# Second chunk's first k and v sums ahead of the raw weight loads, first chunk's loads joined, three high halves on VectorE

## The chip, the cores and the metric

One core of a Trainium2 chip runs the program. TensorE multiplies, VectorE (DVE) and ScalarE (ACT) do elementwise work and reductions, GpSimd (POOL) does some of it and issues accumulating DMAs, SyncE (SP) issues most other DMAs. Every engine works through its own instructions in the order in which they were written out, and waits where one needs something that is not there yet. The metric is the device time of one execution in microseconds; the median of three runs is 759.44 us (757.23 to 761.62).

## The reference

Three layers on 4 sequences of 576 positions, 8 heads of 64 features (512 in all), fp32:

```python
# attention, twice, added
q_d, k_d, v_d = (t.reshape(B, H, 144, 4, D).mean(axis=3) for t in (q, k, v))
out_d = softmax(q_d @ k_d.T / 8) @ v_d                  # every 4th position
out_up = np.repeat(out_d, 4, axis=2)
mask = np.abs(pos[:, None] - pos[None, :]) < 4
out_local = softmax(np.where(mask, q @ k.T / 8, -1e9)) @ v
x = (out_up + out_local).reshape(B, S, 512)
# feed-forward with a norm
xn = (x - mean) / np.sqrt(var + 1e-6) * g_ln
x = x + np.maximum(xn @ w_ch1, 0) @ w_ch2               # 512 -> 2048 -> 512
# mixing with the previous position
k = np.maximum((mu_k * x + (1 - mu_k) * x_prev) @ w_k, 0)   # 512 -> 1024
r = sigmoid((mu_r * x + (1 - mu_r) * x_prev) @ w_r)
out = r * (k * k @ w_v)
```

The sums over four positions (k_d, v_d, q_d without the factor) are the "sums" of this document.

## The kernel before

The 2304 positions are cut into six chunks of 384. For each chunk the attention runs in four units, one for each pair of heads (`hp` 0 to 3; `units` lists them as (chunk, hp)), then the norm, then the feed-forward in 16 blocks of 128 hidden features: `emit_l1` fills a bank `h_ps`, `split_h` writes `hh` (ScalarE, L663) and `hl` (VectorE, L664), `emit_l2` adds into four banks `acc`. While chunk c is in the feed-forward, the units of chunk c+1 are woven in between (`Attn`, `slot`). After six chunks the mixing layer follows. Each fp32 product is made of three passes over high and low parts (`mm3`, L290 to L292).

Weights arrive as raw 64-bit numbers (`raw`, L122, 512 KB a DMA) and are turned into fp32 and then into a high part `w_..h` and a low part `w_..l`. `conv_gen` does this piece by piece: A (two ScalarE passes, L80 and L81), D (one VectorE pass, L83), H (the high half, L86, a copy on ScalarE unless the piece's number stands in `BY_VECTOR`), L (the low half, L89, VectorE). Pieces 0 and 1 are the first quarter of `w1`, 2 and 3 of `w2`, 4 and 5 the second quarter of `w1`, 6 and 7 of `w2`, 8 and 9 the third of `w1`, 10 and 11 of `w2`. Four fetches of two DMAs each run ahead (`AHEAD`).

The first chunk is done by hand, as two pairs of head pairs (`pair(0)`, `pair(1)`) in an order given by the string `FIRST`: a digit is a step of that pair, a dot four idle matmuls, `a` and `b` the v sums, A, D, H, L with a number weight steps, `n` a step of the norm. Its k comes whole (`kf`) and is summed on VectorE (L832), its v comes as four raw rows (`vr_01`) and is summed in L779 and L781.

The later chunks' sums are made by DMAs (`sums`): the first quarter of a k sum `kd` and of a v sum `vd` is loaded by SP, then GpSimd issues three adding DMAs on top, each after the one before has landed (L335, L336). The second chunk needs sums of sequence 1; its units 0 and 1 had theirs issued in step `q` of `FIRST`, after four fetches of raw weights, with their q, k and v loads. A `scd` matmul (L393) multiplies `kd` by the summed q, `sc` (L397) is the windowed score.

Completion of DMAs from SP and ScalarE is told over eight lanes taken in turn (`DMAHW0` to `DMAHW7` in the orders below), and an issue waits for the DMA that had its lane before.

## Time and profile before

| | us |
|---|---|
| median of three runs | 759.44 |
| the profiled execution | 759.42 |
| its span, first to last instruction | 757.6 |
| TensorE busy | 731.2 |
| VectorE busy | 438.8 |
| ScalarE busy | 375.7 |
| GpSimd busy | 106.3 |

The profile is one execution. Its page gives busy times and shares, 40 slices of the span, queues, the chain that ended last and the costliest groups; the trace behind it answers for any stretch with a timeline, lists of waits, windows and DMA queues. A row of a timeline ends with the idle time ahead of it and what ended that, in brackets. Matmuls overlap, so their durations add up to more than the distance of their starts.

### The profile page before, as it was taken

The numbers are of one execution on the slowest core, as the hardware profiler recorded it, in microseconds if no ns is written. First come the engines' busy times: TensorE is split into PE (matmuls) and PEld (weight loads), VectorE is DVE, ScalarE is ACT, GpSimd is POOL, SyncE is SP. The second block draws the span as 40 slices with busy tenths as digits, with TensorE's granted clock in tenths as the row PEclk, the third lists the DMA queues.
The fourth block names the chain that finished last, engine by engine and source line by source line (L and its number), as shares of the span: only waits on it lengthen the run. The fifth ranks groups of instructions, "written<-read, shape, count | busy, mean of one in ns | idle before, by whom it ended". The sixth has DMA issues, their size and how long they took to land.

```text
span 757.6 us, 13995 instructions
## 1 busy us (share of the span) xinstructions
PE 731.2 (97%) x5472; PEld 708.7 (94%) x5472; DVE 438.8 (58%) x820; ACT 375.7 (50%) x782; POOL 106.3 (14%) x141
## 2 busy tenths in 40 slices
PE   4869999999999999999999999999999999999998
PEld 3658899999999999999999999999999999999998
DVE  4986987755475556645675554547797355143211
ACT  1887975535254343544355344236888576411100
POOL 3044200500063404510300020002000000000000
PEclk8798999999999999999999999999999999999999
DMA  9899653464538754755332346906725628695311
GB/s 272 284 305 270 163 152 102 106 205 138 171 98 197 185 165 119 162 136 182 126 111 102 99 131 220 353 33 208 259 105 187 205 94 310 230 295 183 106 63 53
DMA packets 76306, 130.43 MB, mean 172 GB/s; under 512 B 8464, under 2 KB 53136, under 8 KB 74576
## 3 DMA queue, kind: packets, MB, share of 16 engines
q1 hardware_dynamic: 65456, 118.97, 47.7%
q0 software_dynamic: 9920, 9.25, 6.9%
q10 hardware_dynamic: 864, 1.32, 0.6%
q8 instruction: 43, 0.70, 0.4%
q14 instruction: 23, 0.19, 0.1%
HBM read 89.13 MB, written 40.37 MB: 171 GB/s over the span
## 4 chain that ended last, share of the span: by engine, by line
PE 86%; DMA 8%; ACT 4%; issue 0%; SPq 0%; DVE 0%; POOL 0%; DVEq 0%; ACTq 0%
PE b_ps L1166 10%; PE acc L290 9%; PE h_ps L290 8%; PE acc L292 8%; PE acc L291 8%; PE h_ps L291 8%; PE h_ps L292 8%; PE b_ps L291 7%; PE b_ps L290 7%; PE b_ps L292 7%; DMA kd<-in_kr 3%; PE av L469 2%; DMA q<-in_qw 2%; PE sc L397 1%; PE scd L393 1%; DMA vd<-in_vr 1%
## 5 line engine op out<-in xcount | busy, mean ns | idle before, releaser
L663 ACT ACTIVATE hh<-h_ps 128x384 fp32r<-128x384 f32 x96 | 47.0, 490 | 111.9 <-PE h_ps L292 107.4
L664 DVE SCALAR_TENSOR_TENSOR hl<-h_ps,hh 128x384 fp32r<-128x384 f32 x96 | 53.0, 553 | 81.0 <-ACT hh L663 80.4
L1166 PE MATMUL b_ps<-xk,wk 128*128 128x384 f32 x504 | 88.3, 335 | 0.2 <-DVE u L1138 0.2
L1166 PEld LDWEIGHTS b_ps<-xk,wk 128*128 128x128 f32 x504 | 87.3, 188 | 0.8 <-DVE u L1138 0.5
L698 POOL TENSOR_TENSOR x<-x2t,x 128x384 f32<-128x384 f32 x24 | 24.1, 1022 | 296.7 <-DVE x2t L697 296.5
L290 PE MATMUL b_ps<-ko,wv 128*128 128x384 f32 x192 | 64.1, 334 | 0.0
L291 PE MATMUL b_ps<-ko,wv 128*128 128x384 f32 x192 | 64.1, 334 | 0.0
L292 PE MATMUL b_ps<-ko,wv 128*128 128x384 f32 x192 | 64.1, 334 | 0.0
L1292 DVE TENSOR_TENSOR rin<-b_ps,rin 128x384 f32<-128x384 f32 x24 | 13.3, 557 | 61.4 <-PE b_ps L292 60.2
L335 POOL DMA_DIRECT2D kd<-in_kr x36 | 36.4, 1015 | 70.5 <-DMA kd<-in_kr 70.0
L336 POOL DMA_DIRECT2D vd<-in_vr x36 | 37.1, 1032 | 36.3 <-DMA vd<-in_vr 28.2
L83 DVE SCALAR_TENSOR_TENSOR rm<-rm,raw 128x512 uint32<-128x512 uint32 (+1 forms) x40 | 33.7, 844 | 9.3 <-ACT raw L81 9.0
L1218 ACT CAST ko<-kin 128x1536 fp32r<-128x1536 f32 x12 | 17.6, 1478 | 38.9 <-PE b_ps L291 22.9
L291 PEld LDWEIGHTS b_ps<-ko,wv 128*128 128x128 f32 x192 | 36.0, 188 | 0.0
L290 PEld LDWEIGHTS b_ps<-ko,wv 128*128 128x128 f32 x192 | 36.0, 188 | 0.0
L292 PEld LDWEIGHTS b_ps<-ko,wv 128*128 128x128 f32 x192 | 36.0, 188 | 0.0
L80 ACT ACTIVATE rm<-raw 128x512 f32<-128x512 f32 (+1 forms) x40 | 32.6, 815 | 4.1 <-DMA raw<-in_w 1.8
L1220 DVE TENSOR_TENSOR ko<-kin,ko 128x1536 fp32r<-128x1536 f32 x12 | 20.9, 1754 | 23.0 <-ACT ko L1218 22.9
L290 PE MATMUL acc<-hh,w_0h 128*128 128x384 f32 x96 | 33.3, 347 | 0.2 <-ACT w_0h L86 0.2
L290 PE MATMUL acc<-hh,w_1h 128*128 128x384 f32 x96 | 33.4, 348 | 0.0
L290 PE MATMUL h_ps<-ah,w_2h 128*128 128x384 f32 x96 | 33.3, 347 | 0.0
L291 PE MATMUL acc<-hl,w_0h 128*128 128x384 f32 x96 | 32.7, 340 | 0.0
(221 smaller groups left out, 2087.0 us busy)
## 6 DMA issues: line engine op xcount, KB each, us to landing
raw<-in_w SPq DMA_DIRECT2D x32, 512.0 KB, 7.1
kd<-k SPq DMA_DIRECT2D x48, 192.0 KB, 2.1
kin<-kd SPq DMA_DIRECT2D x12, 768.0 KB
wk<-wkd SPq DMA_DIRECT2D x7, 1024.0 KB, 9.4
v<-in_vw SPq DMA_DIRECT2D x20, 256.0 KB, 3.3
rd<-r SPq DMA_DIRECT2D x24, 192.0 KB, 1.9
rin<-rd SPq DMA_DIRECT2D x24, 192.0 KB, 2.6
out<-rin SPq DMA_DIRECT2D x24, 192.0 KB, 3.2
```

Of the source, the lines that this page charges most:

```text
L80: in_order(pinned, nc.scalar.activation(ru.bitcast(F32), high.bitcast(F32), AF.Prelu, scale=-2.0 ** -80, alpha=-2.0 ** -32))
L83: in_order(pinned, nc.vector.scalar_tensor_tensor(ru, ru, 3, low.bitcast(U32), op0=ALU.logical_shift_left, op1=ALU.bitwise_or))
L290: nc.tensor.matmul(ps, wh, ah, start=first, stop=False)
L291: nc.tensor.matmul(ps, wh, al, start=False, stop=False)
L292: nc.tensor.matmul(ps, wl, ah, start=False, stop=last)
L335: in_order(r > 0, eng.dma_start(kd, kr[b, hp, r], **op))
L336: in_order(r > 0, eng.dma_start(vd, vr[b, hp, r], **op))
L663: nc.scalar.activation(hh, ps[:, 0:N], AF.Relu)
L664: last_hl[0] = nc.vector.scalar_tensor_tensor(hl, ps[:, 0:N], 0.0, hh.bitcast(F32), op0=ALU.max, op1=ALU.subtract)
L698: nc.gpsimd.tensor_tensor(x[:, o, :], t, x[:, o, :], op=ALU.add)
L1166: nc.tensor.matmul(ps, a, m[:, k, :], start=start and k + i == 0, stop=k == nk - 1 and i == 2, skip_group_check=True)
L1220: nc.vector.tensor_tensor(l, t[g], h.bitcast(F32), op=ALU.subtract)
```

## The change

The first chunk's q, v and raw v come with one DMA for two head pairs in place of two; `vr` lies in memory with the four raw rows of a position side by side, so that a partition's load is one run of 4 KB. Both pairs' q and k are issued before the mask and the small vectors. The first sums of the second chunk's units 0 and 1 (SP's first quarters and GpSimd's adds) are issued behind the first pair's v and raw v and in front of the raw weights; their q and k loads stand between the second and third fetch of raw weights, and v behind the fourth. Step `q` is gone from `FIRST`. GpSimd's memsets are reordered. The high halves of pieces 5, 8 and 10 are copied by VectorE.

```diff
--- before.py
+++ after.py
@@ -164,6 +164,7 @@
 
         for _ in range(AHEAD):
             fetch()
+            yield
         yield step
         for n in range(len(keys) + 1):
             for ops in ((("H", n - 1), ("A", n)), (("L", n - 1), ("D", n))):
@@ -333,7 +334,7 @@
             for b, kd, vd in new:
                 eng, op = (nc.gpsimd, {"accum_op": ALU.add}) if r else (nc.sync, {})
                 in_order(r > 0, eng.dma_start(kd, kr[b, hp, r], **op))
-                in_order(r > 0, eng.dma_start(vd, vr[b, hp, r], **op))
+                in_order(r > 0, eng.dma_start(vd, vr[b, hp, :, r], **op))
             if new:
                 yield True
 
@@ -760,19 +761,17 @@
 
     def load_pair(pr):
         b = sets[pr]
+        in_order(True, nc.sync.dma_start(b["q"], qw[2 * pr:2 * pr + 2, :, 0:NG].rearrange("i p n w -> p i n w")))
         for i in range(2):
-            in_order(True, nc.sync.dma_start(b["q"][:, i], qw[2 * pr + i, :, 0:NG]))
             in_order(True, nc.scalar.dma_start(b["kf"][:, i], kf[0, 2 * pr + i]))
 
     def load_pair_v(pr):
-        for i in range(2):
-            in_order(True, nc.sync.dma_start(sets[pr]["v"][:, i], vw[2 * pr + i, :, 0:NG]))
+        in_order(True, nc.sync.dma_start(sets[pr]["v"], vw[2 * pr:2 * pr + 2, :, 0:NG].rearrange("i p n h d -> p i n h d")))
 
     vr_01 = [block(2048)[0].rearrange("p (i r f) -> p i r f", i=2, r=4) for _ in range(2)]
 
     def load_pair_vr(pr):
-        for i in range(2):
-            in_order(True, nc.sync.dma_start(vr_01[pr][0:KD, i].rearrange("p r (t d) -> p r t d", t=2), vr[0, 2 * pr + i].rearrange("r p t d -> p r t d")))
+        in_order(True, nc.sync.dma_start(vr_01[pr][0:KD].rearrange("p i r f -> p i (r f)"), vr[0, 2 * pr:2 * pr + 2].rearrange("i p r t d -> p i (r t d)")))
 
     def value_sums(pr):
         t = vr_01[pr][0:KD]
@@ -781,13 +780,10 @@
             in_order(True, nc.vector.tensor_tensor(vdt[0, 2 * pr + i].rearrange("p t d -> p (t d)"), t[:, i, 0], t[:, i, 1], op=ALU.add))
 
     load_pair(0)
+    load_pair(1)
     nc.scalar.dma_start(mask_t, mask)
     for hp in range(NHP):
         sum_tiles(0, hp)
-    for h in range(2):
-        p = slice(64 * h, 64 * h + 64)
-        for i in range(2):
-            nc.gpsimd.memset(kz[i][p, 1 - h], 0.0)
     for b in sets:
         nc.vector.memset(b["qd"][:, :, :, QB:64], 0.0)
         nc.gpsimd.memset(b["P"], 0.0)
@@ -796,19 +792,28 @@
     nc.vector.memset(one, 1.0 / DM)
     nc.scalar.copy(ones_r, one)
     make_identity(nc, ident)
-    load_pair(1)
-    nc.scalar.dma_start(vec_t, vec)
-    for pr in range(2):
-        load_pair_v(pr)
-        load_pair_vr(pr)
-    by_hand = next(conv)
+    load_pair_v(0)
+    load_pair_vr(0)
+    for h in range(2):
+        p = slice(64 * h, 64 * h + 64)
+        for i in range(2):
+            nc.gpsimd.memset(kz[i][p, 1 - h], 0.0)
+            nc.gpsimd.memset(qdz[i][p, :, 1 - h], 0.0)
     for b in sets:
         nc.gpsimd.memset(b["PT"], 0.0)
-    for i in range(2):
-        for h in range(2):
-            p = slice(64 * h, 64 * h + 64)
-            nc.gpsimd.memset(qdz[i][p, :, 1 - h], 0.0)
     nc.gpsimd.memset(PT, 0.0)
+    nc.scalar.dma_start(vec_t, vec)
+    for _ in zip(*[sums(*units[NHP + i]) for i in range(2)]):
+        pass
+    load_pair_v(1)
+    load_pair_vr(1)
+    for n in range(AHEAD):
+        next(conv)
+        if n == 1:
+            for i in range(2):
+                load_qk(*units[NHP + i])
+    load_v(*units[NHP])
+    by_hand = next(conv)
     xt[0] = xp.tile([128, NHP, N], F32, tag="x", name="x")
 
 
@@ -950,12 +955,6 @@
             warm(4)
         elif o == "W":
             warm(WARM, W1[0][0][:, 0, :], 512)
-        elif o == "q":
-            for i in range(2):
-                load_qk(*units[NHP + i])
-            for _ in zip(*[sums(*units[NHP + i]) for i in range(2)]):
-                pass
-            load_v(*units[NHP])
         else:
             next(steps[o], None)
 
@@ -1299,7 +1298,7 @@
 AHEAD = 4
 PINNED = 4
 UB = 2
-BY_VECTOR = ()
+BY_VECTOR = (5, 8, 10)
 PRE = 3
 SB = 8
 KB = 5
@@ -1313,7 +1312,7 @@
 PROB = 800
 PRO0 = 10
 GAP = -1
-FIRST = "0 0 1 1 . . . . 0 0 a 1 0 0 0 1 b A0 0 1 1 D0 1 0 0 H0 1 0 1 A1 A2 1 L0 1 D1 q n W H1 n L1 n D2"
+FIRST = "0 0 1 1 . . . . 0 0 a 1 0 0 0 1 b A0 0 1 1 D0 1 0 0 H0 1 0 1 A1 A2 1 L0 1 D1 n W H1 n L1 n D2"
 EARLY = 0
 IDLE = 2
 WARM = 8
@@ -1338,7 +1337,7 @@
     vwin = vp[:, :, idx, :].reshape(B, NHP, 2, 6, 4, 32, D)
     vwin[..., WIN:, :] = 0
     vwin = vwin.transpose(1, 4, 5, 0, 3, 2, 6).reshape(NHP, 128, 6 * B, 2, D)
-    vr = v.reshape(B, NHP, 2, 2, KD, 4, D).transpose(0, 1, 5, 4, 3, 2, 6).reshape(B, NHP, 4, KD, 2, 128)
+    vr = v.reshape(B, NHP, 2, 2, KD, 4, D).transpose(0, 1, 4, 5, 3, 2, 6).reshape(B, NHP, KD, 4, 2, 128)
     kr = k.transpose(0, 1, 3, 2).reshape(B, NHP, 128, SD, 4).transpose(0, 1, 4, 2, 3)
     vec = np.stack([np.asarray(inputs[n]).reshape(KT, 128).T for n in ("moe_g_ln", "moe2_mu_k", "moe2_mu_r")], axis=1)
```

SP's queue at the start of the program, before. `first_114` and `first_115` are the blocks of the first and second pair (q and k), `first_116` holds v of both, `first_121` and `first_122` raw v. Behind the last row stand six more raw loads, then six loads of q and k, and then the first two `kd`.

```order
L764 DMA first_114<-in_qw 128x416 x2
L764 DMA first_115<-in_qw 128x416 x2
L769 DMA first_116<-in_vw 128x512
L769 DMA first_116<-in_vw 128x512 [waits DMAHW0_49]
L775 DMA first_121<-in_vr 72x4x256 [waits DMAHW2_49]
L775 DMA first_121<-in_vr 72x4x256 [waits DMAHW5_49]
L769 DMA first_116<-in_vw 128x512 [waits DMAHW6_49]
L769 DMA first_116<-in_vw 128x512 [waits DMAHW7_49]
L775 DMA first_122<-in_vr 72x4x256 [waits DMAHW0_49]
L775 DMA first_122<-in_vr 72x4x256 [waits DMAHW1_49]
L122 DMA raw_166<-in_w1 128x1024 [waits DMAHW2_49]
L122 DMA raw_166<-in_w1 128x1024 [waits DMAHW3_49]
```

SP's queue at the same place, now, up to the first load of raw weights:

```order
L764 DMA first_114<-in_qw 128x2x416
L764 DMA first_115<-in_qw 128x2x416
L769 DMA first_116<-in_vw 128x2x512
L774 DMA first_121<-in_vr 72x2x1024
L336 DMA kd_165<-in_kr 128x144 [waits DMAHW2_49]
L337 DMA vd_166<-in_vr 72x256 [waits DMAHW3_49]
L336 DMA kd_169<-in_kr 128x144 [waits DMAHW4_49]
L337 DMA vd_170<-in_vr 72x256 [waits DMAHW5_49]
L769 DMA first_116<-in_vw 128x2x512 [waits DMAHW6_49]
L313 DMA q_193<-in_qw 128x416 [waits DMAHW7_49]
L774 DMA first_122<-in_vr 72x2x1024 [waits DMAHW0_49]
L122 DMA raw_187<-in_w1 128x1024 [waits DMAHW1_49]
```

The four first quarters `kd_165`, `vd_166`, `kd_169` and `vd_170` have moved from behind the eight raw loads to the fifth to eighth place; the second pair's v and raw v moved behind them.

ScalarE's queue of loads at the start, before: `first_114` and `first_115` take the k of the two pairs.

```order
L765 DMA first_114<-in_kf 128x579 x2
L784 DMA mask_t_101<-in_mask 128x240
L797 CAST ones_r_83<-one_146 128x128 [waits DVE_49]
L765 DMA first_115<-in_kf 128x579 [waits DMAHW1_49]
L765 DMA first_115<-in_kf 128x579 [waits DMAHW3_49]
```

And now:

```order
L766 DMA first_114<-in_kf 128x579 x2
L766 DMA first_115<-in_kf 128x579 x2
L784 DMA mask_t_101<-in_mask 128x240 [waits DMAHW0_49]
L793 CAST ones_r_83<-one_144 128x128 [waits DVE_49]
L805 DMA vec_t_81<-in_vec 128x12 [waits DMAHW1_49]
```

The second pair's k stands in front of the mask and waits for no earlier DMA; the mask waits for the first q.

VectorE around the second chunk's first unit, before (`w1_1h` and `w1_1l` are the second quarter of `w1`, `sm`, `mx`, `P`, `T` belong to the unit's softmax):

```order
L423 TENSOR_SCALAR sm_708<-sm_708 96x2
L516 TENSOR_TENSOR sum_l_1494<-xc_580,sum_h_1493 128x384
L424 RECIPROCAL mx_707<-sm_708 96x2 [waits DVE_49]
L429 TENSOR_REDUCE sm_708<-P_112 128x8 [waits Activation_49]
L83 SCALAR_TENSOR_TENSOR rm_799<-rm_799,raw_607 128x1024 [waits DMAHW5_49,DMAHW4_49]
L430 RECIPROCAL mx_707<-sm_708 128x8 [waits DVE_49]
L89 TENSOR_TENSOR w1_1l_665<-rm_666,w1_1h_664 128x1024 [waits Activation_49]
L432 TENSOR_TENSOR P_112<-P_112,mx_707 128x8x30 [waits DVE_49]
L444 STREAM_TRANSPOSE T_790<-P_112 128x256 [waits DVE_49]
```

And now:

```order
L424 TENSOR_SCALAR sm_702<-sm_702 96x2
L86 CAST w1_1h_658<-rm_660 128x1024 [waits DVE_49]
L425 RECIPROCAL mx_701<-sm_702 96x2 [waits DVE_49]
L430 TENSOR_REDUCE sm_702<-P_112 128x8 [waits Activation_49]
L351 TENSOR_REDUCE qdz1_111<-q_197 64x2x48 [waits DMAHW7_49]
L431 RECIPROCAL mx_701<-sm_702 128x8 [waits DVE_49]
L351 TENSOR_REDUCE qdz1_111<-q_197 64x2x48
L433 TENSOR_TENSOR P_112<-P_112,mx_701 128x8x30 [waits DVE_49]
L89 TENSOR_TENSOR w1_1l_659<-rm_660,w1_1h_658 128x1024
L445 STREAM_TRANSPOSE T_784<-P_112 128x256 [waits DVE_49]
```

The cast of piece 5 stands on VectorE behind the unit's sum, in front of the reciprocals, the low half and the transpose; the next unit's q sums (`qdz1_111`) moved in front of the transpose, and the pass `sum_l` behind it.

## Rows read from the trace of the kernel before

**Rows 1.** Busy table of the page, whole run: us (share) xcount per engine

```profile
PE 731.2 (97%) x5472; PEld 708.7 (94%) x5472; DVE 438.8 (58%) x820; ACT 375.7 (50%) x782; POOL 106.3 (14%) x141
```

**Rows 2.** TensorE's waits, whole run: us in total, times, longest us

```profile
PE scd L840 <- DVE kd L832: 10.4, 3, 7.3
PE scd L393 <- DMA kd<-in_kr: 5.8, 1, 5.8
```

**Rows 3.** Timeline, VectorE, 0 to 62: start us, us, operation [idle before, releaser]

```profile
7.84 0.94 DVE L828 TENSOR_REDUCE first<-first 128x192 f32<-128x768 f32 x1
...
12.02 0.76 DVE L832 TENSOR_REDUCE kd<-first 128x144 f32<-128x576 f32 x1 [3.24 <-DMA first<-in_kf]
...
13.90 0.75 DVE L832 TENSOR_REDUCE kd<-first 128x144 f32<-128x576 f32 x1 [1.12 <-DMA first<-in_kf]
...
17.54 1.21 DVE L779 TENSOR_TENSOR first<-first 72x1024 f32<-72x1024 f32 x1
...
58.93 0.45 DVE L403 TENSOR_REDUCE mx<-scd 96x2 f32<-96x288 f32 x1 [5.03 <-PE scd L393]
```

**Rows 4.** Timeline, TensorE, 51 to 81 us

```profile
51.85 0.41 PE L393 MATMUL scd<-kd,qdz 128*96 128x144 f32 x2
...
58.10 0.79 PE L393 MATMUL scd<-kd,qdz 128*96 128x144 f32 x2 [5.84 <-DMA kd<-in_kr]
...
61.87 0.41 PE L290 MATMUL h_ps<-ah,w_0h 128*128 128x384 f32 x1
...
78.46 0.69 PE L393 MATMUL scd<-kd,qdz 128*96 128x144 f32 x4
...
79.63 0.44 PE L292 MATMUL h_ps<-ah,w_1l 128*128 128x384 f32 x1
...
80.95 0.33 PE L290 MATMUL acc<-hh,w_1h 128*128 128x384 f32 x1
```

**Rows 5.** Windows: length, busy us of PE, PEld, DVE, ACT, POOL, clock, DMA, GB/s

```profile
52.00:58.00 6.00, 0.26 (x3) 0.02 (x1) 1.90 (x3) 3.12 (x4) 3.45 (x5) 0.77 0.82 199
...
58.00:62.00 4.00, 3.90 (x41) 3.42 (x42) 2.53 (x6) 1.47 (x6) 2.75 (x4) 0.50 0.79 127
...
70.00:100.00 30.00, 29.49 (x276) 27.36 (x276) 27.01 (x51) 29.38 (x57) 7.11 (x8) 1.00 0.67 192
```

**Rows 6.** DMA queues, 0 to 6 us: packets, MB, share (q1 SP, q10 ScalarE)

```profile
q1 hardware_dynamic: 430, 0.65, 35.8%
q10 hardware_dynamic: 391, 0.69, 30.2%
```

**Rows 7.** DMA totals in 0 to 8, 0 to 13 and 0 to 20 us

```profile
DMA packets 1294, 2.10 MB, mean 262 GB/s; under 512 B 136, under 2 KB 786, under 8 KB 1294
...
DMA packets 2292, 3.41 MB, mean 262 GB/s; under 512 B 255, under 2 KB 1460, under 8 KB 2291
...
DMA packets 3525, 5.58 MB, mean 279 GB/s; under 512 B 424, under 2 KB 2216, under 8 KB 3524
```

**Rows 8.** GpSimd's timeline from 8 us; line L335 in 0 to 95 us

```profile
34.48 1.05 POOL L335 DMA_DIRECT2D kd<-in_kr  x1 [26.32 <-DMA kd<-in_kr]
...
55.35 0.90 POOL L335 DMA_DIRECT2D kd<-in_kr  x1 [0.91 <-DMA kd<-in_kr]
...
DMA to landing us min/median/max: 2.7/6.7/10.3
```

**Rows 9.** Lines L884, L86, L89: engine, count, ns minimum/median/maximum, first and last start

```profile
L884 DVE COPY first<-first x4: 351/354/357, 23.0 to 30.7; 32x384 f32<-32x384 f32 x4
...
L86 ACT CAST w_0h<-rm x4: 1037/1066/1097, 33.2 to 50.7; 128x1024 fp32r<-128x1024 f32 x4
...
L89 DVE TENSOR_TENSOR w_0l<-rm,w_0h x4: 1218/1219/1226, 36.1 to 52.2; 128x1024 fp32r<-128x1024 f32 x4
```

**Rows 10.** Timeline, ScalarE, 26 to 65 us

```profile
26.43 1.14 ACT L80 ACTIVATE rm<-raw 128x1024 f32<-128x1024 f32 x1
...
64.30 0.49 ACT L663 ACTIVATE hh<-h_ps 128x384 fp32r<-128x384 f32 x1 [1.47 <-PE h_ps L292]
```

## The prediction

> **What bounds the kernel now.** I read the busy table first. TensorE is busy 731.2 of 757.6 us [rows 1], so the end moves only if TensorE's idle 26.4 us shrink or its matmuls run at another clock. The list of TensorE's waits, longest first, then says where the idle time is: 10.4 us for the first chunk's k sums and 5.8 us for one k sum of the second chunk [rows 2]. Both lie in the first 60 us; in the 30 us from 70 on TensorE is busy 29.49 us [rows 5], so what is gained before 60 us reaches the end of the program unless it is lost again on the way.
>
> Next, VectorE's timeline. It waits 3.24 and 1.12 us for the second pair's k (the two last L832 rows, at 12.02 and 13.90); from there its rows show hardly an idle mark until 53.9 us, and then stands 5.03 us behind the second chunk's scores [rows 3]. So the first 54 us are VectorE's chain, and what delays it in front delays all of it. TensorE's timeline shows the other hole: two `scd` matmuls start at 51.85 and end at 52.26, the next two start at 58.10, after 5.84 us of waiting for `kd<-in_kr` [rows 4]. The granted clock is 0.77 in 52 to 58 and 0.50 in 58 to 62, that is partly and then wholly the lower of the two levels, after this idle stretch [rows 5].
>
> **The change part by part.**
>
> *First chunk's loads.* Before, the second pair's k goes onto ScalarE's queue at 5.57 and later, since each issue waits for an earlier DMA, and lands at 12.0 and 13.9 [rows 3]. Now all four k loads stand at the head of that queue with no wait, and the two q loads at the head of SP's. In the first 6 us the two queues move 0.65 and 0.69 MB [rows 6], and by 8 us 2.10 MB in all [rows 7]; the two q pairs and the four k loads are 1.99 MB. With equal shares ScalarE's queue lacks 0.47 MB of its 1.16 MB at 6 us; at half of the 380 GB/s between 6 and 8 us ((2.10 - 1.34)/2) that takes 2.5 us: 8.5 us. VectorE ends the second pair's q sum at 8.8 [rows 3] and needs the last k at about 9.5. Both waits go: 3.24 + 1.12 = 4.4 us. The other end: in before the last k landed only when some 3.4 to 3.7 MB, nearly all that had been issued, had moved. If it again comes last among the eight DMAs now in front (3.1 MB), then at the 260 GB/s between 8 and 13 us ((3.41 - 2.10)/5 [rows 7]) it lands at 8 + 1.0/0.26 = 11.9 us; its sum would start then instead of at 13.90, and the gain is 2.0, or 1.6 us with a short wait for the mask behind it. I take 4.4, since the queue rows show equal shares. The Trainium skill (DMA: Bandwidth & Descriptors, Queues, rings and completion order) says that each DMA engine serves the queues in turn, packet by packet; by that the 8.5 us holds, the 11.9 us does not, and the 0.65 to 0.69 MB of the trace agree.
>
> The raw v rows come with 4 KB runs and one DMA per pair; they are needed at 17.54 - 4.4 = 13.1 us [rows 3]. In front of their end stand 3.2 MB: 2.10 at 8 us and 1.1 at 0.26 give 12.2 us. They are hidden by 0.9 us; without it the chain slips by what is lacking. The first raw weights are read on ScalarE at 26.43 [rows 10], 22.0 after the shift; 2.6 MB more stand between (k and v sums' first quarters, v, q, raw v, the raw weights themselves), which at the 0.31 MB/us between 13 and 20 us ((5.58 - 3.41)/7 [rows 7]) is 8.4 us: 20.6 us, hidden. The rearranged memsets on GpSimd keep their sum and cost nothing: they ended at 8 us.
>
> *Second chunk's sums.* Their first quarters now go out on SP in front of the raw weights, in the fifth to eighth place, at about 8 us; behind v and raw v they land at about 13. GpSimd then adds three quarters in rounds, each waiting for the landing of the one before. Before, the first add started at 34.48 and the last began at 55.35 [rows 8]. One add takes 6.7 us to land in the median and 10.3 at most, with about 0.9 us to issue. Three rounds from 13 us end at 13 + 3 x 7.6 = 36, at worst at 13 + 3 x 11.2 = 47 us. TensorE wants the sum at 51.85 - 4.4 = 47.4. So the hole of 5.84 us goes. With it goes the low clock: 58.10 to 61.87 takes 3.77 us for two `scd`, 32 `sc` and six matmuls; at the full clock four `scd` and 32 `sc` take 1.17 (78.46 to 79.63), of which the two missing `scd` are 0.3, and seven matmuls 1.32 (79.63 to 80.95), so six 1.13 [rows 4]: 2.0 in all. 1.8 us come back; at worst none, if the clock falls for another reason.
>
> *What is given back.* During the hole ScalarE worked 3.12 us and VectorE 1.90 [rows 5], mostly on weights; that work now runs beside TensorE. ScalarE's slack at its next join is 1.47 us (`hh` at 64.30 [rows 10]). In 70 to 100 us ScalarE is busy 29.38 and VectorE 27.01 of 30 us [rows 5], so there is little room to catch up. The three high halves leave ScalarE, 3 x 1.07 us, and come to VectorE [rows 9]. VectorE's price for one is not in the trace: its own copy of 384 columns takes 0.354 us, so in proportion 0.94; the lower end is 0.35 and the upper end a two-operand pass over 1024 columns, 1.22. I take 0.94, from the row of the same operation: 2.8 us more on VectorE, of which two casts fall in 70 to 100 us and raise it to 28.9 of 30, while ScalarE falls to about 27.2. The Trainium skill (VectorE: DVE Perf Modes, The perf-mode tier table) gives a one-source fp32 copy in SBUF two elements a cycle and a two-source operation one; with its fixed part that is an estimate of 0.69 us, 2.1 us for the three. The copy row, shorter than the two-operand rows of its width, agrees in direction; the sum would change by less than a microsecond.
> I put what TensorE loses at its joins (transposes of `Pd`, `PT`, the first use of each weight part) at 3.12 - 1.47 = 1.7 for ScalarE's lost lead, and 0.3 for the moved casts: 2.0 us. Bounds: 0, and 4.5 if the lead and a cast's upper price are paid in full.
>
> *Sum.* 4.4 + 5.8 + 1.8 - 2.0 = 10.0 us less. The profiled execution took 759.42 us (span 757.6, 1.8 around it), equal to the median 759.44 of the runs shown: 749.4 us. Ends: 1.6 + 5.8 + 0 - 4.5 = 2.9 gives 756.5, and 12.0 with another 1 us of slack gives 746.4.
>
> **Rivals.** *Nothing is given back.* The casts unload ScalarE, which ran 29.38 of 30 us, and every microsecond reaches the end: 4.4 + 5.8 + 1.8 = 12.0, 747.4 us. For it: after the hole TensorE had next to no wait with a fuller ScalarE. Against: those two engines had the hole to work ahead.
>
> *The second pair's k comes no sooner*, being last in its queue once more, and the joins cost their upper end: 1.6 + 7.6 - 4.5 = 4.7, 754.7 us. For it: total rate fell to 260 GB/s from 8 us on [rows 7]. Against: the equal shares.
>
> *The gain is eaten by VectorE.* With 28.9 to 29.5 of 30 us busy, `hl`, which TensorE needs for every feature block, queues behind casts and weights, and each of some twelve blocks between 50 and 100 us waits for three quarters of a cast, 0.7 us: 8.4 us more than the 10.0 forecast leave, so 757.8, no change. For it: the fill. Against: in 70 to 100 us it still had 3.0 us free, and two casts take 1.9 of them.
>
> *Slower: the adds starve behind the raw weights.* They now run while SP's queue is full from 13 us on, where before the first ones met a lull. If the last add lands at X, TensorE waits X - 47.8 us, and the low clock returns: the change is -4.4 + (X - 47.8) - 5.8 + 2.0. It breaks even at X = 56.0 and is 0.5% (3.8 us) slower from X = 59.8, that is at (59.8 - 13)/3 = 15.6 us a round; at 16.5 it is 62.5 and 6.5 us slower, 765.9. For it: one queue against a saturated one. Against: in 44 to 55 us the adds already ran beside raw weights, and no landing took over 10.3 us [rows 8].
>
> **Chances.** The forecast, 7 to 11.5 us less, 0.60; nothing given back 0.13; k no sooner, or half of the gain, 0.15; eaten, within 3.8 us, 0.08; slower 0.04. Half a percent, 3.8 us, is about what a measurement of this kernel can tell from no change. Faster by more: 0.60 + 0.13 + 0.15 = 0.88; same 0.08; slower 0.04. Range 746.0 to 756.5: the forecast, nearly all of the second and most of the third case.
>
> **What would show it.** VectorE's second pair of k sums starts at about 8.8 us with no wait for `in_kf`, and the chain behind is some 4.4 us early; GpSimd's first add starts near 13 us; the first `scd` of the second chunk stands at about 47 us with no wait for `kd<-in_kr`, and the clock stays at its upper level from 46 us on; three casts of L86 stand on VectorE at 0.7 to 0.95 us. It is wrong if the k sums wait until 12 us, if TensorE's waits name `kd` again, or if new waits for `Pd`, `PT`, `hl` or a weight part between 50 and 100 us add up to more than 4.5 us.

## The result and the profile after

The changed kernel took 751.26 us in the median of four runs (750.39 to 753.31), against 759.81 us of the kernel before on the same chip: a ratio of 0.9894, 95% interval 0.9858 to 0.9929. Two later comparisons of the same kernel gave 0.9894 (0.9878 to 0.9910) and 0.9902 (0.9879 to 0.9926); over all 14 runs the median is 751.6. That is 8.1 to 8.6 us less than before, where 10.0 were forecast, and inside the range.

The execution profiled took 753.31 us, the longest of its four (span 751.5); that is 6.1 us less than the profiled execution of before. It is read first, and a shorter one of the same kernel beside it further down. Line numbers are those of each kernel; the same work stands up to five lines further down in the changed one. TensorE's waits (us in total, times, longest us) answer to [rows 2]:

```profile
PE scd L845 <- DVE kd L837: 7.9, 2, 6.9
PE tp L895 <- ACT first L886: 4.6, 2, 3.7
PE h_ps L676 <- ACT ah L544: 2.6, 1, 2.6
```

The wait for the second chunk's `kd` is gone from the list, and a new one of 2.6 us stands at the first product of the feed-forward, `h_ps` at L676. The wait at `tp` was 2.0 us in before; those products start 1.2 us sooner now (21.81 against 22.98), so what was added to it costs nothing there. In before, the first product waited 1.25 us, and the last of its three passes ended at 45.20:

```profile
40.27 2.13 PE L675 MATMUL h_ps<-ah,w_0h 128*128 128x384 f32 x8 [1.25 <-ACT ah L543]
...
43.65 1.55 PE L675 MATMUL h_ps<-al,w_0h 128*128 128x384 f32 x8
```

From 50 to 100 us of the changed kernel only 0.6 us of TensorE's waits are left:

```profile
PE tp L460 <- ACT Pd L427: 0.4, 1, 0.4
PE scd L394 <- DVE x L488: 0.2, 1, 0.2
```

VectorE's timeline in the first chunk (start us, us, operation, in brackets the idle time before it and who ended it) answers to [rows 3]:

```profile
8.82 0.75 DVE L837 TENSOR_REDUCE kd<-first 128x144 f32<-128x576 f32 x1
11.31 0.75 DVE L837 TENSOR_REDUCE kd<-first 128x144 f32<-128x576 f32 x1 [1.74 <-DMA first<-in_kf]
...
14.12 0.72 DVE L871 TENSOR_TENSOR P<-sc,mask_t 128x240 f32<-128x240 f32 x2 [1.13 <-PE sc L852]
```

The third k sum waits no more; the last still does and starts 2.59 us earlier than the 13.90 of before. At the addition of the mask (L871) 1.13 us of that go again. TensorE's timeline around the second chunk's start answers to [rows 4]:

```profile
35.32 2.30 PE L360 MATMUL idle<-w_0h 128*128 128x512 f32 x8
40.24 3.12 PE L676 MATMUL h_ps<-ah,w_0h 128*128 128x384 f32 x8 [2.62 <-ACT ah L544]
43.16 1.97 PE L676 MATMUL h_ps<-ah,w_0l 128*128 128x384 f32 x8
44.96 1.55 PE L676 MATMUL h_ps<-al,w_0h 128*128 128x384 f32 x8
...
53.17 0.65 PE L394 MATMUL scd<-kd,qdz 128*96 128x144 f32 x4
...
55.45 0.33 PE L291 MATMUL h_ps<-ah,w_0h 128*128 128x384 f32 x1
...
72.32 0.73 PE L394 MATMUL scd<-kd,qdz 128*96 128x144 f32 x4 [0.21 <-DVE x L488]
```

The four score matmuls now run in one piece, but they start at 53.17, which is 1.3 us later than the 51.85 of [rows 4]. The second unit's scores start at 72.32 instead of 78.46. The windows (length, busy us of PE, PEld, DVE, ACT, POOL, clock, DMA, GB/s) show the clock; the last one compares with the 70 to 100 of [rows 5], moved by the time gained:

```profile
41.00:44.00 3.00, 3.00 (x10) 3.00 (x11) 3.00 (x5) 2.40 (x4) 0.89 (x1) 0.50 1.10 321
52.00:58.00 6.00, 6.00 (x65) 5.72 (x64) 5.97 (x10) 6.00 (x12) 1.63 (x2) 1.00 0.86 238
58.00:62.00 4.00, 3.60 (x22) 3.25 (x20) 3.67 (x11) 4.00 (x8) 1.14 (x2) 1.00 0.97 318
63.00:93.00 30.00, 29.75 (x277) 27.95 (x276) 28.93 (x50) 27.25 (x53) 5.66 (x6) 1.00 0.67 196
```

The clock is 1.00 in the three windows behind 52 us, where [rows 5] had 0.77 and 0.50; there is a new stretch at 0.50, 41 to 44 us, in the first product. What held that product back stands on ScalarE's timeline; its first row answers to the first of [rows 10], where ScalarE did not wait:

```profile
25.77 1.15 ACT L80 ACTIVATE rm<-raw 128x1024 f32<-128x1024 f32 x1 [0.64 <-DMA raw<-in_w]
...
36.60 1.14 ACT L80 ACTIVATE rm<-raw 128x1024 f32<-128x1024 f32 x1 [1.32 <-DMA raw<-in_w]
...
39.57 2.13 ACT L544 ACTIVATE ah<-xc,vec_t 128x384 fp32r<-128x384 f32 x4
```

Twice ScalarE waits for a raw weight, and `ah` (L544), which the first product needs, stands behind it in ScalarE's order.

Two more profiles of the same kernel belong beside this one (`r_after` and `r_after2` below). In `r_after2` ScalarE had no such wait, and TensorE's rows at the same places are:

```profile
38.78 2.14 PE L676 MATMUL h_ps<-ah,w_0h 128*128 128x384 f32 x8 [1.25 <-ACT ah L544]
40.76 1.55 PE L676 MATMUL h_ps<-ah,w_0l 128*128 128x384 f32 x8
42.15 1.55 PE L676 MATMUL h_ps<-al,w_0h 128*128 128x384 f32 x8
...
50.36 0.65 PE L394 MATMUL scd<-kd,qdz 128*96 128x144 f32 x4
```

Its first product starts 1.5 us before that of the kernel before, at the full clock, and its span is 748.5. The pair shows that one profile of a kernel whose executions differ by 3 us is one of its outcomes, not the kernel.

All profiles are in the table below; times in us, "score 1" and "score 2" are the starts of the second chunk's first and second score matmuls, "rest" is the span less score 2, and the median is over the runs measured together with that profile.

| kernel | last k sum | first product | clock 41 to 44 | score 1 | score 2 | span | rest | median |
|---|---|---|---|---|---|---|---|---|
| before | 13.90 | 40.27 | 1.00 | 51.85 | 78.46 | 757.6 | 679.1 | 759.4 to 760.2 |
| changed | 11.31 | 40.24 | 0.50 | 53.17 | 72.32 | 751.5 | 679.2 | 751.3 |
| r_after | 11.07 | 39.89 | 0.63 | 53.04 | 72.19 | 750.7 | 678.5 | 752.1 |
| r_after2 | 11.22 | 38.78 | 1.00 | 50.36 | 69.48 | 748.5 | 679.0 | 751.8 |
| e1 old loads | 15.63 | 42.12 | 1.00 | 53.72 | 72.82 | 751.4 | 678.6 | 752.7 |
| e2 loads only | 11.20 | 40.08 | 1.00 | 51.65 | 72.94 | 752.4 | 679.5 | 760.3 |
| r_e2 | 11.47 | 38.70 | 1.00 | 50.29 | 77.52 | 756.7 | 679.2 | 758.9 |
| e3 no casts | 11.58 | 40.24 | 1.00 | 51.84 | 71.42 | 751.1 | 679.7 | 752.4 |
| e4 mask first | 14.02 | 40.39 | 1.00 | 51.96 | 71.06 | 750.0 | 678.9 | 752.6 |
| e5 raw first | 11.10 | 38.46 | 1.00 | 50.05 | 69.11 | 748.9 | 679.8 | 750.9 |
| r_e5 | 10.90 | 38.64 | 1.00 | 50.20 | 69.29 | 748.0 | 678.7 | 750.8 |
| e6 mask on GpSimd | 10.26 | 40.71 | 1.00 | 52.28 | 71.38 | 750.9 | 679.5 | 752.2 |
| e8 six casts | 11.53 | 40.54 | 1.00 | 52.13 | 68.84 | 754.2 | 685.4 | 755.3 |
| e9 more idle products | 10.91 | 41.85 | 0.83 | 54.84 | 73.96 | 753.4 | 679.4 | 751.3 |

The rest is 678.5 to 679.8 us in thirteen of the fourteen, with and without the hole, with no cast or three on VectorE. In these the end follows the start of score 2, and the table splits an execution into what came before it and what did not matter. e8, with six casts on VectorE, is the exception: its score 2 is the earliest of all, because that matmul stands earlier in TensorE's order there, and its rest is 6 us longer. The marker holds only as long as the order of work behind it stays much the same.

### The profile page after: what moved, and what is told of

It reads as the page before. It is cut to its first block, busy times and chain, and to the rows that moved or that the text cites. A ratio compares the mean times of both kernels' runs of the same rounds, so it can differ in the third digit from the quotient of the medians.

```text
span 751.5 us, 13982 instructions
## 1 busy us (share of the span) xinstructions
PE 728.4 (97%) x5472; PEld 707.0 (94%) x5472; DVE 440.6 (59%) x823; ACT 373.5 (50%) x779; POOL 106.4 (14%) x141
## 4 chain that ended last, share of the span: by engine, by line
PE 87%; DMA 7%; ACT 3%; SPq 1%; DVE 1%; issue 1%; ACTq 0%; DVEq 0%
PE b_ps L1165 9%; PE acc L291 9%; PE h_ps L291 9%; PE acc L293 8%; PE acc L292 8%; PE h_ps L293 8%; PE h_ps L292 8%; PE b_ps L291 7%; PE b_ps L293 7%; PE b_ps L292 7%; DMA raw<-in_w 3%; PE av L470 2%; DMA kz<-in_kw 2%; DMA first<-in_vr 2%; PE sc L398 1%; PE scd L394 1%
## 5 line engine op out<-in xcount | busy, mean ns | idle before, releaser
L449 ACT COPY PT<-T 32x192 f32<-32x192 f32 x80 | 28.0, 350 | 10.5 <-DVE T L445 9.7
```

What stands on the lines that cost most here:

```text
L449: nc.scalar.copy(PT[p, :, j, :], T[p, :, 0:24])
```

## The experiments

**e1_old_loads: the sums and casts without the new first loads.** The core of the edit to the changed kernel, shortened:

```diff
-        in_order(True, nc.sync.dma_start(b["q"], qw[2 * pr:2 * pr + 2, :, 0:NG].rearrange("i p n w -> p i n w")))
         for i in range(2):
+            in_order(True, nc.sync.dma_start(b["q"][:, i], qw[2 * pr + i, :, 0:NG]))
...
-    load_pair(1)
     nc.scalar.dma_start(mask_t, mask)
...
+    load_pair(1)
     nc.scalar.dma_start(vec_t, vec)
```

> The changed kernel with the first chunk's loads as they were (four loads of q, two k loads, then the mask, the other two k loads; v and raw v in pairs, ordered as before); the sums in front of the raw weights and the three casts on VectorE stay. Theory A (the trace after: the first chunk's lead of 2.6 us is eaten before the second chunk begins, and the whole gain is the closed hole and its clock, 7.5 us): last k lands near 13.9 instead of 11.3, VectorE's wait on the mask's place is gone, the raw weights land no later than the work on them; the second chunk's first score matmul starts at 52 to 54 us as in the changed kernel (53.2), no wait for kd, and the time is 750 to 753 us. Theory B (the recorded prediction: the loads are worth 4.4 us, less 2.0 given back): 755 to 757 us, the score matmul at 55 us or later.

Measured: 752.73 us, ratio to before 0.9924 (0.9906 to 0.9941), no wait for kd, score 1 at 53.72. That is theory A's time, and 2 us or more under theory B's. The sums in front of the raw weights, with the casts, give about 7.0 us (759.75 less 752.73), though score 1 is 1.9 us later than in before. One detail missed: the last k sum started at 15.63, not 13.9. With the old loads the front of the program is 1.7 us worse than before, and the changed kernel's last k sum is 4.3 us ahead of it, yet the median differs by 1.1 us only. Why the front is later with the old loads stays open.

**e2_loads_only and r_e2: the new first loads without the sums and casts**, run twice. The joined loads are those of the change; the rest of the edit to the kernel before, shortened:

```diff
     load_pair(0)
+    load_pair(1)
     nc.scalar.dma_start(mask_t, mask)
...
-    load_pair(1)
     nc.scalar.dma_start(vec_t, vec)
```

> The kernel before with only the joined and reordered loads of the first chunk; the second chunk's sums stay behind the raw weights and the casts on ScalarE. Theory A (the raw weights' lateness in the changed kernel comes from the loads and sums put in front of them): raw weights land as early as before, so the lead of about 2.6 us less 1.1 at the mask carries on, the first product of the MoE starts near 38.8 instead of 40.3, with the clock at 1.00 behind it; but kd is late as before (near 57.7), so the hole grows from 5.8 to about 7.3 us and the time stays at 759 to 760.5. Theory B (the loads themselves give 4.4): first product near 36, the hole 9 to 10 us, the time still 758 to 760. If instead the joined loads delay the raw weights by themselves, the first product starts at 40 or later.

Measured: 760.3 us, ratio 1.000 (0.9979 to 1.0021). Both theories have the time, neither the trace: the one execution profiled was the shortest of twelve (754.23) and had 2.26 us of hole. Its first product, at 40.08, fits the last sentence of the expectation, but ScalarE waits for no raw weight in that profile. So it was profiled again:

> The kernel before with only the joined and reordered loads of the first chunk, again: its first profile was of its shortest execution (754.2 us against a median of 760.3) and showed a hole of only 2.26 us at the second chunk's scores. The span has been 679 to 680 us behind the second unit's first score matmul in every profile. Theory A (kd comes late in most executions whatever the first chunk's loads do, and an earlier start only lengthens the wait for it): at a time of 759 to 761 the second unit's score matmul starts at 78 to 80 us, the first at 50.3 to 52, and the hole between its halves is 6 to 8.5 us. Theory B (the loads cure the hole and something else costs the 6 us): hole under 3 us at a time of 759 or more, with the loss in another place.

Measured: 758.85 us, ratio 0.9994 (0.9975 to 1.0013); the profiled execution, at 758.46, is near the median. TensorE's rows:

```profile
38.70 2.14 PE L675 MATMUL h_ps<-ah,w_0h 128*128 128x384 f32 x8 [1.24 <-ACT ah L543]
...
50.29 0.41 PE L393 MATMUL scd<-kd,qdz 128*96 128x144 f32 x2
57.39 0.80 PE L393 MATMUL scd<-kd,qdz 128*96 128x144 f32 x2 [6.69 <-DMA kd<-in_kr]
...
77.52 0.68 PE L393 MATMUL scd<-kd,qdz 128*96 128x144 f32 x4
```

Theory A holds in the main: of the lead of 1.56 us at score 1 (50.29 against 51.85) 0.85 go into a hole of 6.69 instead of 5.84 us, and score 2 is 0.94 earlier than in before, a little under the 78 to 80 expected. The loads alone are worth nothing that can be told in the median, because kd is late for another reason. The lowest and the typical execution also show how the time hangs on the hole: 2.26 us of it at 754.2, 6.69 at 758.5. They show the clock's part as well: behind the short hole the granted clock stayed at 1.00 (54 to 58 us), behind the long one it was 0.53 (57 to 61 us).

**e4_mask_first: the mask between the two pairs' k loads.**

```diff
+    nc.scalar.dma_start(mask_t, mask)
     load_pair(1)
-    nc.scalar.dma_start(mask_t, mask)
```

> The changed kernel with the mask's load issued between the two pairs' k loads, where the kernel before had it. Theory A1 (the wait of 1.13 us at VectorE's addition of the mask is for the mask, which is issued last of the early loads): that addition starts within 0.2 us of the work ahead of it, near 13.0 to 13.4 instead of 14.1; the last k lands up to 0.3 us later; the raw weights still come late, so at most 0.5 us of it reaches the end: 750.5 to 751.5 us. Theory A2 (it waits for TensorE's score matmuls, as the trace's releaser says): the wait stays at 1 us or more and the time is that of the changed kernel.

Measured: 752.62 us, ratio 0.9924 (0.9904 to 0.9943), above the time of either theory. VectorE's rows:

```profile
14.02 0.75 DVE L837 TENSOR_REDUCE kd<-first 128x144 f32<-128x576 f32 x1 [2.56 <-DMA first<-in_kf]
...
15.65 0.72 DVE L871 TENSOR_TENSOR P<-sc,mask_t 128x240 f32<-128x240 f32 x2
```

The wait at the mask's addition is gone, as A1 says, though the releaser named in the changed kernel was TensorE; in e2 and e5 the same row names `DMA mask_t<-in_mask`. The other half of A1 is wrong: the last k sum is not 0.3 but 2.7 us later, at 14.02, as late as in before. ScalarE's issues say why; first the changed kernel's, then e4's (start us, us, issues):

```profile
0.76 2.46 ACTq L766 DMA_DIRECT2D first<-in_kf  x4
```

```profile
2.26 3.26 ACTq L766 DMA_DIRECT2D first<-in_kf  x2
```

With four k loads and two q loads in front, all are issued without a wait, by 3.22 us, and the mask is the first that has to wait for an earlier DMA to end (issued at 5.28). Put the mask in between, and the fourth k load waits in its place: the last two k issues end at 5.52. So nearly all of the 2.6 us that k gains comes from its place in front of the mask; e4 has the joined loads too, and k is as late as before. The price is 1.1 us at the mask.

**e5_raw_first and r_e5: the second chunk's q and k behind eight raw pieces instead of four.**

```diff
         next(conv)
-        if n == 1:
-            for i in range(2):
-                load_qk(*units[NHP + i])
+    for i in range(2):
+        load_qk(*units[NHP + i])
```

> The changed kernel with the second chunk's q and k loads issued behind the first eight pieces of raw weights instead of behind the first four. Theory A (late raw weights, 0.6 and 1.3 us of wait on ScalarE, hold up the first product, whose late start costs the clock for another 1.3 us): ScalarE's second wait goes, the first product starts at 39.2 to 39.8 instead of 40.2, TensorE is at clock 1.00 at 41 to 44 us instead of 0.50, the second chunk's first score matmul starts near 51 instead of 53.2, and the time falls by 1.5 to 2.5 us against the changed kernel (749 to 750). If q and k of the second chunk come late instead, a wait shows at the matmuls on kz and the gain is lost. Theory B (what is before the second chunk does not set the time): no change, within 0.5 us.

Measured: 750.92 us, ratio 0.9900 (0.9879 to 0.9922). What theory A says of the trace came out, and more: one wait of 1.11 us for the raw weights, no second one, first product at 38.46, clock 1.00, score 1 at 50.05. The time did not: 749 to 750 were said. Against the profiled execution of the changed kernel that is 2.6 us of span (748.9 against 751.5). But the medians differ by 0.3 us, so it was run again beside the changed kernel:

> The kernel with the second chunk's q and k behind the first eight raw pieces, again, beside the changed kernel and the one with more idle products. Theory A (no second wait for raw weights, so no idleness and no low clock; first product at 38.5 to 39): 750 to 751, 1 to 1.5 us under the changed kernel. Theory B (the first profile was a lucky execution): as the changed kernel, within 0.5 us.

Measured: 750.82 us, ratio 0.9892 (0.9867 to 0.9916), trace as in the first (first product 38.64, score 1 at 50.20); r_after2 on the same chip 751.83. Over all runs, 12 against 14, the medians are 750.9 and 751.6. Raw weights in front do keep the first product early in both profiles, but the gain in the median, 0.7 us, is less than the runs of one kernel differ (749.75 to 754.16). It is the shortest version by median; that it beats the changed kernel is not shown.

**r_after and r_after2: the changed kernel again.**

> The changed kernel as it is, again, for a second profile and a tighter time. The five profiles so far give the span as 678.6 to 679.8 us behind the start of the second chunk's second unit (its first score matmul). Theory A (the late raw weights and the low clock at 41 to 44 us of the first profile happen in every execution): the first product starts near 40.2 us again at clock 0.50, that score matmul at 72 to 72.5, and the span is 751 to 752. Theory B (they are the mark of that one execution, the longest of its four, 753.3 us): the first product starts at 38.5 to 39.5 us at clock 1.00, the score matmul at 70 to 70.7, the span is 749 to 750 and the median 750.5 to 751.5.

> The changed kernel as it is, third time, for a comparison on the same chip. Expected by both theories: 751.3 to 752.1 us; by the theory of the late raw weights a third profile with ScalarE's wait of 1.1 to 1.4 us near 36.3 us, the first product near 40 and a clock under 0.7 at 41 to 44.

Measured: 752.07 and 751.83 us. The first profile repeats the late raw weights (0.68 and 1.17 us on ScalarE, clock 0.63, score 1 at 53.04), the second does not (no wait, clock 1.00, score 1 at 50.36). Both theories are half right: it is no mark of one execution, and it doesn't happen in every one. SP's rows show what differs. Of the first profile of the changed kernel (start us, us, issues; below, a wait in total, times, longest):

```profile
22.59 1.97 SPq L317 DMA_DIRECT2D kz<-in_kw  x2
...
25.71 3.17 SPq L122 DMA_DIRECT2D raw<-in_w  x2
```

```profile
SPq L317 <- DMA first<-in_vr: 2.5, 1, 2.5
```

And of r_after2:

```profile
20.34 1.75 SPq L317 DMA_DIRECT2D kz<-in_kw  x2
...
23.50 5.00 SPq L122 DMA_DIRECT2D raw<-in_w  x4
```

```profile
SPq L317 <- DMA first<-in_vr: 0.7, 1, 0.7
```

The raw pieces behind the second chunk's k are issued at 25.71 in the one and at 23.50 in the other. In front of them a load of that k waits for the second pair's raw v to land, 2.5 us in the one and 0.7 in the other. The other profiles with the same order of loads agree: with 2.6 us of this wait (r_after), 2.4 (e8) and 3.4 (e9) ScalarE's second wait is there, with 0.9 (e3) it is not. Why that one load, issued at 14.0 to 14.4 us in the three profiles of the changed kernel, lands near 22.5 in two of them and near 20.3 in the third stays open.

**e3_no_casts and e8_more_casts: none, or six, of the high halves on VectorE.**

```diff
-BY_VECTOR = (5, 8, 10)
+BY_VECTOR = ()
```

> The changed kernel with all casts of the high halves on ScalarE, as before. Theory A (nothing is given back behind the second chunk's start, with the casts or without): the median is that of the changed kernel within 0.8 us, and the span again 679 us behind the second unit's first score matmul. Theory B (ScalarE's lead is what the casts save): 1 to 3 us slower, with new waits of TensorE for ScalarE at 60 to 90 us. Theory C (the recorded term: the casts cost VectorE's lead): 0.3 to 1 us faster.

Measured: 752.36 us beside 752.07 of the changed kernel: theory A within what can be told. From score 1 to score 2 it takes 19.58 us, against 19.06 to 19.15 in all the profiles with three casts and no hole, and 0.3 us of wait for `w_1h` is new. From score 1 to the end it is 699.3, against 697.7 to 698.9 in those profiles. In this one profile the casts are worth some 0.5 to 1 us; the medians show no difference.

```diff
-BY_VECTOR = (5, 8, 10)
+BY_VECTOR = (5, 6, 7, 8, 9, 10)
```

> The changed kernel with six high halves (pieces 5 to 10) on VectorE in place of three (5, 8 and 10). Each takes 0.65 to 0.68 us there, so VectorE has 2.0 us more to do at 55 to 90 us, where it is busy 28.93 of 30 us already. Theory A (VectorE's queue has room to give, and nothing is given back): same median within 0.8 us. Theory B (VectorE is at its edge there): 1 to 2 us slower, with waits of TensorE for VectorE at 60 to 90 us.

Measured: 755.28 us, 3.2 more than the changed kernel on the same chip and more than theory B has. TensorE's waits from 50 to 140 us:

```profile
PE av L470 <- ACT PT L449: 1.2, 1, 1.2
PE var L520 <- DVE x L488: 1.0, 1, 1.0
```

TensorE's busy time from 80 to 90 us is 8.59 us where r_after has 9.94, and from 100 to 120 18.99 where it has 20.00. The first wait names ScalarE's copy `PT`, which itself waits for VectorE's transpose, with a cast of 0.69 us (78.62) just in front of it. So six casts are too many for VectorE and three are not. The edit also moves later work, the second chunk's scores among it, to other places in the order, and how much of the 3.2 us that costs was not separated.

**e6_mask_pool: e5 with the mask's load issued by GpSimd at the start.**

```diff
+    nc.gpsimd.dma_start(mask_t, mask)
     load_pair(0)
     load_pair(1)
-    nc.scalar.dma_start(mask_t, mask)
```

> The changed kernel with the second chunk's q and k behind the first eight raw pieces and the mask's load issued by GpSimd at the very start, so that all four k loads still go out at once and the mask no longer stands behind them. Theory A (k and the mask are late only through their place among the loads in flight): last k at 11.1 to 11.5 us, no wait for the mask at its addition, which starts near 12.8 instead of 13.7; ScalarE's wait for the first raw piece grows by the same 0.9 to 2.0, so the first product starts at most 0.5 us earlier than 38.46, and the time is 750 to 751. Theory B (ScalarE's wait does not matter): the whole 0.9 us reaches the first product, 37.6, and the time is 749.5 to 750.

Measured: 752.16 us, ratio 0.9889 (0.9870 to 0.9909). The front did what theory A says and more: last k sum at 10.26, the mask's addition at 11.89 without a wait. Then ScalarE's and TensorE's rows:

```profile
26.03 1.12 ACT L80 ACTIVATE rm<-raw 128x1024 f32<-128x1024 f32 x1 [3.13 <-DMA raw<-in_w]
```

```profile
28.51 2.01 PE L894 MATMUL tp<-ident,first 128*72 128x128 f32 x8 [3.15 <-ACT first L885]
...
31.06 1.55 PE L905 MATMUL av<-first 128*64 128x96 f32 x16 [0.21 <-ACT first L896]
```

The whole lead of 1.8 us is spent waiting for the first raw piece, which comes at 26.0 as in e5. Worse, TensorE then stands idle for 3.15 us where e5 had 1.03, and its products behind it, at a granted clock of 0.50 (28.5 to 33 us), take 1.55 us where e5's, at 1.00, take 0.88. The first product is at 40.71, 2.2 us later than in e5. Neither theory had that; the shorter front did not shorten the program in the median, though one of the six executions, 748.93 us, was the shortest of all kernels here.

**e9_warm: 14 idle products in front of the first product instead of 8.**

```diff
-WARM = 8
+WARM = 14
```

> The changed kernel with 14 instead of 8 idle products of 128x512 in front of the first product of the MoE (each 0.29 us, so they end near 39.2 us instead of 37.4 to 37.7). Theory A (the clock of 0.50 to 0.63 at 41 to 44 us in both profiles of the changed kernel follows TensorE's 2.5 us of idleness before that product, and costs what the three passes take longer, 5.9 to 6.3 us instead of 5.0): idleness falls to at most 1 us, the clock at 41 to 44 is 1.00, the second chunk's first score matmul starts near 52 instead of 53.1, and the time falls by 0.9 to 1.3 us to 750.3 to 751. Theory B (the clock there has another cause, or what is gained is lost behind it): clock or time as in the changed kernel, 751.3 to 752.1.

Measured: 751.29 us, against 751.83 of the changed kernel, no difference that can be told. The profiled execution was the longest of seven (755.2), with 1.89 and 1.50 us of wait for raw weights; TensorE was idle for 1.88 us before the first product, and the clock was 0.83 at 41 to 44. Idle times before that product of 2.62, 2.48 and 1.88 us went with a low clock, but 2.07 (e8) and 1.65 us (e3) did not. The raw weights came late in this profile and theory A's condition, at most 1 us of idleness, was not met, so it is not tested. More idle products gave no gain that can be told, and what decides the clock there stays open.

## Why the prediction was right, and where it was not

**The hole and its clock: right.** kd's first quarters went out ahead of the raw weights, GpSimd's first add started at 14.77 (13 were said):

```profile
14.77 1.05 POOL L336 DMA_DIRECT2D kd<-in_kr  x1 [6.97 <-DMA kd<-in_kr]
...
36.25 0.89 POOL L336 DMA_DIRECT2D kd<-in_kr  x1 [1.23 <-DMA kd<-in_kr]
```

The last kd add of the two units was issued by 37.1 and the last of all by 38.4. With the 7.3 us that a kd transfer takes to land in the median of that stretch, the last sums were there at about 45 (an estimate; 36 were said, 47 at worst), before 53. The hole is gone in every kernel that has the new order of the sums. From score 1 to the end of the span it took 705.75 us before (757.6 - 51.85) and 698.3, 697.7 and 698.1 in the three profiles of the changed kernel: 7.7 us less in the mean, against 5.8 + 1.8 = 7.6 in the sum. All of it lies in one short stretch: from score 1 to the first `h_ps` product behind it took 10.02 us before (51.85 to 61.87, [rows 4]) and takes 2.28 now (53.17 to 55.45) for the same matmuls, 7.74 less. e1, where the loads stay as they were, has 697.7 from score 1 on and is 7.0 us faster in the median.

**What is given back: the step failed, by 2.0 us.** It was put at "3.12 - 1.47 = 1.7 for ScalarE's lost lead, and 0.3 for the moved casts". But 7.7 against 7.6 leaves nothing given back, so this half of the rival of that name came true. The new waits of TensorE between 50 and 100 us add up to 0.6 us, where before, without the hole, had 0.5. A lead that an engine loses costs only if somebody waits for that engine later; ScalarE filled 6.00 of 6.00 us in 52 to 58, and TensorE waited no longer for it than before. VectorE's timeline of the changed kernel has the casts' price:

```profile
59.60 0.68 DVE L86 CAST w_1h<-rm 128x1024 fp32r<-128x1024 f32 x1
...
80.91 0.65 DVE L86 CAST w_2h<-rm 128x1024 fp32r<-128x1024 f32 x1
```

A cast takes 0.65 to 0.68 us, not 0.94. If a line runs through it and the copy of 384 columns (0.354 us), some 0.17 us of either do not grow with the width; that is an estimate from two rows of different shapes. The estimate of 0.69 us worked out from the Trainium skill (VectorE: DVE Perf Modes, The perf-mode tier table) was the better figure. The rival "eaten by VectorE" did not come; three casts more do cost time in e8, though TensorE's waits there stand behind a transpose and at `x`, not at `hl`.

**The first chunk's loads: the step failed, by 4.7 us in the mean.** 4.4 us were to arrive at score 1; there arrived -1.3, -1.2 and +1.5 in the three profiles. It failed at three places in a row.

1. "8.5 us" for the last k was 11.1 to 11.3. The equal shares were read from [rows 6], but a queue that runs dry shows no share: by 6 us of before, ScalarE's had moved 0.69 MB of the 0.72 that its first two k loads and the mask hold, and from 6 to 8 us it moved (packets, MB, share)

```profile
q1 hardware_dynamic: 426, 0.72, 99.6%
q10 hardware_dynamic: 47, 0.04, 7.0%
```

In the first 6 us of the changed kernel the queues did not move equal shares but 0.76 MB on SP's (q1) and 0.56 on ScalarE's (q10):

```profile
q1 hardware_dynamic: 474, 0.76, 44.3%
q10 hardware_dynamic: 263, 0.56, 24.3%
```

From 6 to 9 us the shares were equal (0.61 and 0.58 MB, at 393 to 395 GB/s), so the bytes account for about 1 us. (The four k loads are 1.19 MB; the sum's 1.16 took the page's KB for thousandths of its MB.) Then ScalarE's queue slowed, with little left to move: 0.09 MB from 9 to 10 us and 0.04 from 10 to 11.2, while the core's rate fell to 281 and 215 GB/s. Why is open; the sum had 380 GB/s and equal shares to the end. The gain there is 2.6 to 2.8 us, nearer to the low end (2.0) than to the 4.4. The sentence drawn from the Trainium skill (DMA: Bandwidth & Descriptors, Queues, rings and completion order), that each engine serves the queues in turn, did not carry the equal shares that I hung on it: in the first 6 us neither the bytes nor the packets (474 and 263) were equal.

2. The mask, named only as "a short wait" at the other end, costs 1.13 to 1.15 us, since it now stands behind all k loads and waits for an earlier DMA (e4). What is left is 1.5 us, and this is what r_after2 and r_e2 show at score 1.

3. "20.6 us, hidden" for the first raw weights was 25.6 to 25.8 in two of three profiles; in the third they were there by 24.96, when ScalarE took them without a wait. I had counted bytes, 2.6 MB at 0.31 MB/us, and not that SP issues in order, each issue waiting for an earlier DMA to end. SP's waits from 8 to 16 us in the first profile:

```profile
SPq L336 <- DMA first<-in_vw: 2.5, 1, 2.5
SPq L313 <- DMA first<-in_vr: 1.8, 1, 1.8
```

These 4.3 us stand in front of the first raw weight's issue, which came at 14.81 (12.38 in the chain of before). The good execution has nearly as much there, 4.0 us; what it lacks is the 1.8 us more that the later raw pieces lose behind the second pair's raw v. In the two profiles with late raw weights ScalarE loses 1.8 to 2.0 us, `ah` is late, and the clock falls in the first product: in the first profile its three passes end 1.3 us later than in before, though they start at the same time. e5 takes the second wait away and has the first product at 38.5 and 38.6. The first pair's raw v, said to land at 12.2, landed at 13.98 and was still hidden: VectorE took it at 16.14 without a wait.

So the total came near by luck, because two errors offset each other: the front gave between -1.3 and +1.5 us instead of +4.4, the part behind gave 7.7 instead of 5.6. In r_after2's execution, the good case, 750.3 us is 0.9 above the forecast. The rival "k no sooner and the joins at their upper end" has the right first half, and its second did not come; the slower rival never came near: the last adds were issued 15 us before score 1.

## What to carry to other kernels

A wait that goes away in front of a stage that is fed by one in-order queue of loads is worth only what the queue's next item allows: ask for the issue time of that item, wait by wait, and not for the bytes in front of it. Closing the hole gave 7.7 us because everything it needed had long landed; opening the front gave 0 to 1 us in the median. In e2 against before, over half of the lead went into a longer wait for kd (r_e2); in the changed kernel against e1 the raw weights came too late in two of three profiles, and an earlier start then left TensorE idle for longer, at the price of its clock. Where executions of one kernel differ by as much as the terms in dispute, profile it two or three times and look for one row whose time sets the end as long as the order of work behind it stays the same, here the second unit's first score matmul.

## What was not expected of the hardware

- One load of 120 KB issued before the fourth k load moves that load's landing by 2.7 us (e4), because the k load behind it then has to wait for a DMA to end before it is issued (by 5.52 instead of 3.22 us).
- In the first 14 us the rate does not hold: 393 to 403 GB/s between 4 and 8 us, 210 between 10 and 14, with the DMA engines 0.86 and 0.95 busy, while the first pair's raw v on 72 partitions was under way (SP saw it landed at 13.98). That the one causes the other is not shown.
- A lead can turn into a loss: in e6 the work came 1.8 us earlier to a wait that ended at the same time as before, TensorE was idle for 3.15 instead of 1.03 us, and the products behind it took 1.55 instead of 0.88 us. Which idle stretches bring the clock down (1.88 us in e9, but not 2.07 in e8) is open. It can fall late: in r_after the first pass behind 2.48 us of idleness still took 2.26 us, and the second 2.76 where the full clock takes 1.55.
- A hole of 2.26 us in the second chunk's first scores left the clock at 1.00 (e2), holes of 5.84 and 6.69 us were followed by 0.50 and 0.53 (before, r_e2).
